# One VectorE operation per head for the row maximum and the copy of the scores to SBUF, the exponentials' bias on GpSimd, fixed PSUM tiles, and new order lists, in a thresholded attention followed by a gated MLP

## The chip, the cores and the metric

The kernel runs on one core of a Trainium2 chip. The core has a TensorE (PE), a VectorE (DVE), a ScalarE (ACT), a GpSimd (POOL) and a SyncE (SP), whose queue issues most of the DMAs. Each engine works through its own queue in order and waits on semaphores for the others. The metric is the device time of one execution in microseconds (us), the median over several runs.

## What is computed

```python
def _attn_ref(q, k, v, tau):                      # 8 batches, 8 heads, 576 rows, 64 wide
    scores = (1.0 / np.sqrt(64)) * np.matmul(q, k.transpose(0, 1, 3, 2))
    thresh = np.max(scores, axis=-1, keepdims=True) - tau          # tau = 0.02
    scores = np.where(scores >= thresh, scores, -1000000000.0)
    scores = scores - np.max(scores, axis=-1, keepdims=True)
    attn = np.exp(scores)
    attn = attn / (np.sum(attn, axis=-1, keepdims=True) + 1e-09)
    return np.matmul(attn, v)

def _moe_ref(x, w_in, w_spatial, b_spatial, w_out):  # x: heads side by side, 512 wide
    h = np.maximum(x @ w_in, 0.0)
    u, v = h[..., :512], h[..., 512:]
    v_n = (v - mean(v)) / np.sqrt(var(v) + 1e-06)
    v_s = np.einsum('ts,bsd->btd', w_spatial, v_n) + b_spatial[None, :, None]
    return (u * v_s) @ w_out
```

Only scores within tau of their row's maximum keep a weight; the weights are normalised by the sum of those kept.

## The kernel before

**Groups.** The 64 heads are taken in 32 pairs, and the rows of a pair in blocks of 128 (the last 64 rows of two pairs share a block), which makes 144 groups of 128 rows x 2 heads x 576 scores, 18 to a batch. A group `g` goes through these steps, each named by a letter in the order lists:

- `S`, `Y` (`scores`, `scores_end`, both through `part`, L819): PE multiplies, and the scores land in one of two PSUM tiles, `s_ring[g % 2]`, each three banks long.
- `G` (`turn_bank`, L834): an empty instruction of ACT, DVE or POOL that hands the middle bank from the one head to the other.
- `M` (`top`, L853): DVE takes the maximum of both heads in one reduction over 128x1152 scores in PSUM and writes it, negated, into a corner of the same PSUM tile.
- `B` (`shift`, L859): DVE turns it into `negm`, the exponentials' bias (maximum, scale and threshold in one), two numbers a row.
- `E`, `F` (`spread`): ACT reads the scores of a head from PSUM with that bias and writes one of three SBUF tiles, `e_ring[g % 3]`. `WAYS` says in which of two ways. In way `n` it is an exponential into fp16 (L874), after which `C` (`keep`, L896) makes a bit mask of what is at least 1 and `A` (`pick`, L905) applies it, both on DVE. In way `a` it is a Prelu in fp32 with a huge slope below the threshold (L877), after which `Z` (`exps`, L912) takes the exponential of both heads on ACT. Either way the weights end in fp16 in `p_ring`. Of the 144 groups 48 go by `n` and 96 by `a`.
- `T` (`turn_p`, L917): a DMA transposes the weights; `RP` does it on PE for a few.

`P`, `i`, `p` (L494 to L537) multiply the transposed weights with V, whose extra column of ones gives the sums, and DVE divides. The result is turned (`X`, `XP`) and goes through the MLP one batch later: `v` (L645), `u` (L712), `s` (L741), `o` (L770).

**Around it.** `QA`, `QB`, `QR` transpose q and k on PE (L437, L456); `qa`, `qb`, `qr` copy the result from PSUM to SBUF on ACT or, with a `d` in front, on DVE (`evict`, L409 to L419). POOL rearranges the loaded q, k and v (L296, L323, L329), copies a 64x64 block for each pair (L449) and normalises the MLP's `v` (L685 to L697).

**Order.** Nothing schedules at run time: `ORDER` has one list of tokens for each batch (`E6:1` is step `E` of group 6 of the batch before), and the program is issued in just that order, so that the lists fix what stands behind what in every engine's queue. `LAST` does the same for the end.

**PSUM.** Six of eight banks hold the two score tiles (pool `ps_s`). The other two (`ps_f`, tiles `f`) take all other products in turn, through `bank`. After the last scores `ps_s` is closed and its six banks serve the end as tiles `t`.

The score tile of group `g` is therefore written by PE, read by DVE, written in a corner and read again by DVE, read twice by ACT, and then written by PE for group `g + 2`.

Of the kernel before, what the change touches and what calls it, by code (L numbers as in the profile page):

```python
# [9 lines left out]
F32 = mybir.dt.float32  # L10
# [24 lines left out]
(  # L35
# [18 lines left out]
(  # L54
# [120 lines left out]
WAYS = [  # L175
    "nananaanananaaanaa",
    "naaaaanananaaanaaa",
    "anaaaaannnaaaaanaa",
    "aaaannnanaaaaaanaa",
    "aaaaaannannnaanaaa",  # L180
    "anaaannannanaanaan",
# [1065 lines left out]
```

## Time and profile before

| | before |
|---|---|
| median of 3 runs | 434.13 us |
| lowest, highest | 432.89, 435.9 us |
| profiled execution | 432.44 us, its span 430.4 us |
| mean granted clock of TensorE | 0.996 |
| instructions in the profile | 12955 |
| ACT, busy share of the span | 381.8 us (89%), 575 instructions |
| POOL, busy share of the span | 170.6 us (40%), 374 instructions |
| HBM read, written | 32.79 MB, 9.44 MB |

The span is the part of the execution that the profile covers; 2.0 us of the profiled execution lie outside it. The profile gives the busy time of each engine, groups of like instructions (with count, busy time, mean length of one, and what the engine waited for ahead of them), waits by who waited for whom, and a timeline. `PEld` is TensorE's weight load, which runs beside the matmuls. A busy time is a union: where the next instruction begins before the one ahead of it has ended, the overlap counts once.

### The profile page before, as it was taken

How to read it: one execution, taken by the hardware profiler on the slowest of the kernel's cores; microseconds unless marked ns; L12 is line 12 of the kernel's file. 1: busy time of each engine (PE TensorE's matmuls, PEld its weight loads, DVE VectorE, ACT ScalarE, POOL GpSimd, SP SyncE). 2: the span in 40 equal slices, each digit the busy share in tenths (PEclk: the TensorE clock that was granted, in tenths of full speed). 3: DMA queues.
4: the chain of work that ended last, by engine and by line, in shares of the span. 5: the costliest groups of instructions: out<-in, count | busy, mean ns of one | idle time of the engine just before them, and what ended most of it. 6: DMA issues, size and time to landing. Idle time of an engine off the chain costs nothing.

```text
span 430.4 us, 12955 instructions
## 1 busy us (share of the span) xinstructions
PE 411.2 (96%) x5028; PEld 252.6 (59%) x5028; DVE 380.0 (88%) x693; ACT 381.8 (89%) x575; POOL 170.6 (40%) x374
## 2 busy tenths in 40 slices
PE   7688899999999999999999999999999999999995
PEld 3456665566745566575664667555665656564742
DVE  6989999989989989989899999998889998999662
ACT  4989999999999998999998999989999989999262
POOL 1263455483117513481334720467024540265020
PEclk9989999999999999999999999999999999999999
DMA  7998999999999999999989999999999999688823
GB/s 198 255 237 177 223 256 220 200 197 218 223 221 213 230 230 234 230 173 277 205 171 238 227 204 185 200 204 241 245 209 181 175 229 212 150 135 215 158 75 120
DMA packets 224700, 88.16 MB, mean 205 GB/s; under 512 B 195648, under 2 KB 220352, under 8 KB 224640
## 3 DMA queue, kind: packets, MB, share of 16 engines
q1 hardware_dynamic: 224192, 86.75, 99.6%
q8 instruction: 40, 0.66, 0.6%
q10 hardware_dynamic: 368, 0.33, 0.2%
q0 software_dynamic: 80, 0.26, 0.2%
q14 instruction: 20, 0.16, 0.1%
HBM read 32.79 MB, written 9.44 MB: 98 GB/s over the span
## 4 chain that ended last, share of the span: by engine, by line
PE 72%; DVE 11%; ACT 8%; issue 4%; DMA 2%; POOL 2%; DVEq 0%; POOLq 0%; ACTq 0%
PE s L819 28%; DVE s L853 7%; PE f L741 6%; PE f L499 5%; PE f L712 5%; PE f L437 5%; PE f L645 4%; PE f L770 4%; ACT e L874 3%; ACT e L877 2%; PE f L494 2%; PE f L630 2%; DMA xT<-xn 1%; PE f L456 1%; DMA uT<-in_moe_w_spatial_dram 1%
## 5 line engine op out<-in xcount | busy, mean ns | idle before, releaser
L853 DVE TENSOR_REDUCE s<-s 128x2 f32<-128x1152 f32 x144 | 195.9, 1361 | 19.5 <-PE s L819 17.0
L819 PE MATMUL s<-qkT 64*64 64x416 f32 (+1 forms) x2304 | 177.8, 417 | 9.6 <-ACT e L874 5.4
L819 PEld LDWEIGHTS s<-qkT 64*64 64x64 f32 x2304 | 105.0, 132 | 67.9 <-ACT e L877 14.5
L877 ACT ACTIVATE e<-s,negm 128x576 f32<-128x576 f32 x192 | 132.5, 741 | 6.6 <-DVE negm L859 4.2
L912 ACT ACTIVATE p<-e 128x1152 f16<-128x1152 f32 x96 | 111.3, 1167 | 0.8
L874 ACT ACTIVATE e<-s,negm 128x576 f16<-128x576 f32 x96 | 66.3, 739 | 8.3 <-DVE negm L859 6.9
L499 PE MATMUL f<-v,pT 128*128 128x65 bf16 x984 | 44.3, 194 | 0.0
L499 PEld LDWEIGHTS <-pT 128*128 128x128 f16 x1024 | 41.8, 98 | 1.9
L323 POOL CAST v<-vl 128x512 bf16<-128x512 f32 x32 | 21.3, 666 | 52.2 <-PE s L819 38.0
L449 POOL COPY qkT<-qkT 64x64 f32<-64x64 f32 x32 | 8.6, 269 | 83.2 <-DVE qkT L413 31.1
L905 DVE TENSOR_TENSOR p<-e 128x576 int32<-128x576 int32 x48 | 39.4, 824 | 0.7 <-PE s L819 0.4
L296 POOL COPY qn<-ql 128x512 f32<-128x512 f32 x31 | 21.1, 681 | 32.3 <-PE s L819 30.8
L741 PE MATMUL f<-wsT,vn 128*128 128x512 bf16 x135 | 33.0, 380 | 0.5 <-DVE xn L537 0.5
L712 PE MATMUL f<-xT,w_in 128*128 128x512 bf16 x116 | 29.6, 380 | 0.0
L697 POOL TENSOR_SCALAR vn<-vrel,rs,nm 128x512 bf16<-128x512 f32 (+1 forms) x35 | 27.7, 792 | 3.6
L645 PE MATMUL f<-w_in,xT 128*128 128x512 bf16 x112 | 28.1, 380 | 0.7 <-ACT vrel L654 0.5
L494 PE MATMUL f<-v,pT 128*128 128x130 bf16 x123 | 27.3, 222 | 0.5 <-DVE xn L537 0.5
L537 DVE TENSOR_TENSOR xn<-f,r 128x384 bf16<-128x384 f32 x46 | 24.8, 548 | 0.8 <-PE s L819 0.3
L770 PE MATMUL f<-w_o,gT 128*128 128x512 bf16 x100 | 25.4, 380 | 0.0
L859 DVE TENSOR_SCALAR negm<-s 128x2 f32<-128x2 f32 x144 | 22.2, 154 | 3.0 <-PE s L819 0.2
L896 DVE TENSOR_SCALAR e<-e 128x1152 uint16<-128x1152 f16 x48 | 23.0, 481 | 0.0
L296 POOL COPY kn<-kl 128x512 f32<-128x512 f32 x31 | 20.4, 657 | 6.0 <-DMA kl<-in_k_dram 6.0
(171 smaller groups left out, 533.6 us busy)
## 6 DMA issues: line engine op xcount, KB each, us to landing
vl<-in_v_dram SPq DMA_DIRECT2D x16, 512.0 KB, 5.6
kl<-in_k_dram SPq DMA_DIRECT2D x15, 512.0 KB, 4.6
ql<-in_q_dram SPq DMA_DIRECT2D x15, 512.0 KB, 5.1
out_dram<-oo SPq DMA_DIRECT2D x12, 512.0 KB, 3.7
pT<-p SPq DMA_TRANSPOSE x141, 4.4
uT<-in_moe_w_in_dram SPq DMA_DIRECT2D x3, 512.0 KB, 5.6
uT<-in_moe_w_spatial_dram SPq DMA_DIRECT2D x2, 576.0 KB, 4.5
vx<-in_v_dram SPq DMA_DIRECT2D x16, 64.0 KB, 4.3
```

The source lines that it names most:

```text
L296: nc.gpsimd.tensor_copy(out=t, in_=ld_ring[i // 2 % 2][w][:, 2 * (i % 2):2 * (i % 2) + 2].rearrange("p h c d -> p c h d"))
L499: nc.tensor.matmul(out=t[:, at + 65 * h:at + 65 * h + 65], lhsT=pt[:, 5 * h + j, rows], rhs=vt[:, 6 * h + j, :], start=False, stop=(h == 1 ...
L645: nc.tensor.matmul(out=t, lhsT=x_of(b, f, slice(c * P, (c + 1) * P)), rhs=w_in[:, f, 512:1024], start=(f == 0), stop=(f == 3))
L712: nc.tensor.matmul(out=t, lhsT=w_in[:, m, f * P:(f + 1) * P], rhs=x_of(b, m, slice(0, 512)), start=(m == 0), stop=(m == 3))
L741: nc.tensor.matmul(out=t, lhsT=vn[:, c, f * P:(f + 1) * P], rhs=wsT[:, c, 0:512], start=(c == 0), stop=(c == 4))
L770: nc.tensor.matmul(out=t[:n], lhsT=gs[b][:, f, c * P:c * P + n], rhs=w_o[:, f, :], start=(f == 0), stop=(f == 3))
L819: made.append(nc.tensor.matmul(out=s_ring[g % 2][halves[k], at[h] + lo:at[h] + hi], lhsT=qks[n][halves[h], 0, m:m + 64], rhs=qks[n][halves ...
L853: nc.vector.tensor_reduce(out=nm[:, heads], in_=view(s_ring[g % 2], at[h0], dims), axis=AX.X, op=ALU.max, negate=True)
L874: nc.scalar.activation(out=half_e(g)[0][:, S * h:S * h + S], in_=s, func=ACT.Exp, bias=bias_, scale=scale if steps[g][1] == 4 else 1.0)
L877: nc.scalar.activation(out=e, in_=s, func=ACT.Prelu, bias=bias_, scale=scale if steps[g][1] == 4 else 1.0, alpha=1e30)
L905: nc.vector.tensor_tensor(out=numerators(g).bitcast(I32), in0=e.bitcast(I32), in1=kept.bitcast(I32), op=ALU.bitwise_and)
L912: nc.scalar.activation(out=numerators(g), in_=e_ring[g % 3].rearrange("p h s -> p (h s)"), func=ACT.Exp)
```

## The change

**Maximum and copy.** For each head DVE issues one `tensor_tensor_reduce`: it adds a broadcast zero to the scores in PSUM, writes the sum (the scores) in fp32 into the SBUF tile of `e_ring`, and keeps the maximum, which goes to a small SBUF tile `peak`. Each of them is built as two instructions, the operation and one that reads the accumulator out. So a group has four instructions of DVE here where it had two.

**Bias.** `shift` runs on POOL, from `peak`, with the sign in its scale.

**Exponentials.** `spread` reads the scores from `e_ring`, in place, and no longer touches PSUM. The fp16 halves of `e_ring` are laid out by head, so that L896 and L905 see two pieces of 576 in place of one of 1152.

**PSUM.** The eight banks are fixed tiles; `next_bank` hands out the two `f` banks in turn, and at the end the banks of the score tiles.

**Lists.** All of `ORDER`, `LAST` and most of `WAYS` are different. 43 groups go by way `n` and 101 by `a`. Of the copies from PSUM, 19 move from ACT to DVE: 12 of `qkT` (15 on DVE before, 27 now), three of `pT`, two of `xT`, one of `wsT`, one of `uT`. PE, POOL (but for the 144 biases) and SP issue the same operations as before in another order; there are 282 on SP before and after.

```diff
 ORDER = [(
-    "S0:0 vG0:0 Y0:0 sk1:0 L3:-1 M0:0 B0:0 L8:0 L7:0 S1:0 aG1:0 Y1:0 M1:0 B1:0 F0:0 E0:0 QR1:0 QB1:0 qr1:0 "
+    "S0:0 G0:0 Y0:0 M0:0 B0:0 F0:0 E0:0 Ci0:0 L7:0 L8:0 S1:0 vG1:0 Y1:0 M1:0 QA1:0 S2:0 sk1:0 G2:0 Y2:0 "
...
-    ps_f = ctx.enter_context(tc.tile_pool(name="ps_f", bufs=2, space=PSUM))
-    ps_s = inner.enter_context(tc.tile_pool(name="ps_s", bufs=1, space=PSUM))
-    s_ring = [ps_s.tile([P, 1536], F32, name=f"s{i}") for i in range(2)]
+    ps = ctx.enter_context(tc.tile_pool(name="ps", bufs=1, space=PSUM))
+    s_ring = [ps.tile([P, 1536], F32, name=f"s{i}") for i in range(2)]
+    f_ring = [ps.tile([P, 512], F32, name=f"f{i}") for i in range(2)]
+    def next_bank(kind):
+        n = in_turn[kind]
+        in_turn[kind] += 1
+        if kind == "f":
+            return f_ring[n % 2][:, 0:512]
+        return s_ring[n % 6 // 3][:, 512 * (n % 3):512 * (n % 3) + 512]
...
 def top(g, heads=slice(0, 2)):
-        nc.vector.tensor_reduce(out=nm[:, heads], in_=view(s_ring[g % 2], at[h0], dims), axis=AX.X,
-                                op=ALU.max, negate=True)
+        for h in range(heads.start, heads.stop):
+            nc.vector.tensor_tensor_reduce(
+                out=e_ring[g % 3][:, h, :], in0=view(s_ring[g % 2], at[h], [[1, S]]),
+                in1=zero.broadcast_to([P, S]), scale=1.0, scalar=float("-inf"),
+                op0=ALU.add, op1=ALU.max, accum_out=peak[g][:, h:h + 1])
 def shift(g):
-        nc.vector.tensor_scalar(out=nm, in0=s_ring[g % 2][:, 704:706],
-                                scalar1=scale if steps[g][1] == 4 else 1.0,
+        nc.gpsimd.tensor_scalar(out=nm, in0=peak[g],
+                                scalar1=-(scale if steps[g][1] == 4 else 1.0),
 def half_e(g):
-        t = e_ring[g % 3].rearrange("p h s -> p (h s)").bitcast(F16)
-        return t[:, 0:1152], t[:, 1152:2304]
+        t = e_ring[g % 3].bitcast(F16)
+        return t[:, :, 0:S], t[:, :, S:2 * S]
 def spread(g, h):
-        s = view(s_ring[g % 2], at[h], [[1, S]])
+        s = e_ring[g % 3][:, h, :]
...
-        inner.close()
-        wide.append(ctx.enter_context(tc.tile_pool(name="ps_t", bufs=6, space=PSUM,
-                                                  reuse_waits="tile")))
+        wide.append(True)
```

DVE's queue from the reduction of group 60 on, in the fourth batch, before (`s_94` and `s_95` are the two score tiles, `e_103` to `e_105` the three tiles of `e_ring`, `p_` those of `p_ring`):

```order
L853 TENSOR_REDUCE s_94<-s_94 128x2
L905 TENSOR_TENSOR p_114<-e_104 128x576
L859 TENSOR_SCALAR negm<-s_94 128x2
L853 TENSOR_REDUCE s_95<-s_95 128x2
L859 TENSOR_SCALAR negm<-s_95 128x2
L896 TENSOR_SCALAR e_103<-e_103 128x1152
L896 TENSOR_SCALAR e_105<-e_105 128x1152
L905 TENSOR_TENSOR p_115<-e_105 128x576
L853 TENSOR_REDUCE s_94<-s_94 128x2
L859 TENSOR_SCALAR negm<-s_94 128x2
```

The same queue from the same group on, in the changed kernel (`s_91` and `s_92` are the score tiles, `f_93` and `f_94` the other two banks; `ISA` is the new operation, and the `ISA` that writes `peak` alone its accumulator read):

```order
L862 ISA e_103,peak<-s_91,zero 128x576
L862 ISA peak 128x1
L862 ISA e_103,peak<-s_91,zero 128x576
L862 ISA peak 128x1
L769 TENSOR_TENSOR gT<-f_94,uT 128x512
L425 TENSOR_SCALAR qkT<-f_93 128x512
L862 ISA e_104,peak<-s_92,zero 128x576
L862 ISA peak 128x1
L862 ISA e_104,peak<-s_92,zero 128x576
L862 ISA peak 128x1
L427 COPY qkT<-f_94 128x512
L427 COPY oo<-f_93 128x512
```

The reduction and the bias of a group have become four instructions in a row, the bias has left the queue, and copies of `qkT` stand between the groups.

POOL's queue around one conversion of v (`v_131`) in the fourth batch, before:

```order
L685 TENSOR_SCALAR rs<-mv 128x1
L690 TENSOR_TENSOR rs<-rs,mhalf 128x1
L692 TENSOR_SCALAR nm<-mv,rs 128x1
L697 TENSOR_SCALAR vn_132<-vrel,rs,nm 128x512
L323 CAST v_131<-vl_139 128x2x4x64
L329 CAST v_131<-vx_143 64x64 x2
```

The queue around the same conversion in the changed kernel (L870 is the bias):

```order
L711 TENSOR_SCALAR vn_132<-vrel,rs,nm 128x512
L870 TENSOR_SCALAR negm<-peak 128x2
L306 COPY qn<-ql_134 128x512
L306 COPY kn<-kl_135 128x512
L870 TENSOR_SCALAR negm<-peak 128x2 x3
L333 CAST v_131<-vl_139 128x2x4x64
L339 CAST v_131<-vx_143 64x64 x2
```

The biases stand singly or in runs between the conversions of q, k and v and the MLP's normalisation.

More of the change, by code (lines that the diff above doesn't have):

```diff
@@ L20 @@
 ORDER = [(
[14 rows of a table removed]
-(
[18 rows of a table removed]
-(
[18 rows of a table removed]
-(
[18 rows of a table removed]
-(
[17 rows of a table removed]
-(
[18 rows of a table removed]
-(
[17 rows of a table removed]
-(
[16 rows of a table removed]
[14 rows of a table added]
+(
[18 rows of a table added]
+(
[19 rows of a table added]
+(
[17 rows of a table added]
+(
[18 rows of a table added]
+(
[18 rows of a table added]
+(
[17 rows of a table added]
+(
[17 rows of a table added]
 LAST = [(
-    "u3:2 eu3:2 s0:2 s1:2 T12:1 es0:2 B16:1 C15:1 A15:1 OUT3:3 sv2:1 es1:2 T13:1 E17:1 s3:2 F17:1 "),
+    "sv3:1 B16:1 E17:1 F17:1 s3:2 T13:1 es1:2 "),
 (
[4 rows of a table removed]
[3 rows of a table added]
 (
@@ L177 @@
     "naaaaanananaaanaaa",
[L178 to L181, printed above, removed]
-    "anaaaanaananaaanan",
-    "anaaaanananaaaanan",
+    "anaaaaannnaanaaaaa",
+    "aaaaaananannaaaaaa",
+    "naanaaanannnaanaaa",
+    "aaaaannaananaaanaa",
+    "aanaaanaaaanaanaaa",
+    "naaaaaanaanaannnaa",
 ]
@@ L224 @@
     sqr = ctx.enter_context(tc.tile_pool(name="sqr", bufs=1))
-    inner = ctx.enter_context(ExitStack())
-    ps_f = ctx.enter_context(tc.tile_pool(name="ps_f", bufs=2, space=PSUM))
-    ps_s = inner.enter_context(tc.tile_pool(name="ps_s", bufs=1, space=PSUM))
-    s_ring = [ps_s.tile([P, 1536], F32, name=f"s{i}") for i in range(2)]
+    ps = ctx.enter_context(tc.tile_pool(name="ps", bufs=1, space=PSUM))
+    s_ring = [ps.tile([P, 1536], F32, name=f"s{i}") for i in range(2)]
+    f_ring = [ps.tile([P, 512], F32, name=f"f{i}") for i in range(2)]
+    in_turn = {"f": 0, "t": 0}
+    def next_bank(kind):
[4 more added lines that the diff above has]
+        return s_ring[n % 6 // 3][:, 512 * (n % 3):512 * (n % 3) + 512]
     identf = const.tile([P, P], F32, name="identf")
@@ L237 @@
     mhalf = const.tile([P, 1], F32, name="mhalf")
+    zero = const.tile([P, 1], F32, name="zero")
     warm = const.tile([P, P], BF16, name="warm")
@@ L388, with shaped @@
     turn = [0]
+    def shaped(t, dtype, n):
+        return t if dtype == F32 else t.bitcast(dtype)[:, 0:n]
     def bank(dtype=F32, n=512):
@@ L394, in bank @@
             if turn[0] % 8 not in (2, 3):
-                return wide[0].tile([P, n], dtype, name="t")
-        return ps_f.tile([P, n], dtype, name="f")
+                return shaped(next_bank("t"), dtype, n)
+        return shaped(next_bank("f"), dtype, n)
     def bank16():
@@ L468, in first @@
         qkt = qk_of(0)
-        tr, tq, tm = (ps_f.tile([P, 512], F32, name="f") for _ in range(3))
+        tr, tq, tm = (next_bank("f") for _ in range(3))
         def turn(t, at, w, c):
@@ L839, in scores_end @@
         follow(part(g, 1, 0, S - cut)[0], turned[g])
-    negm = {}
+    negm, peak = {}, {}
     def top(g, heads=slice(0, 2)):
-        if on_act(g):
-            nm = s_ring[g % 2][:, 704:706]
-        elif g in negm:
-            nm = negm[g]
-        else:
-            nm = negm[g] = small.tile([P, 2], F32, name="negm")
-        h0, n = heads.start, heads.stop - heads.start
-        dims = [[at[1] - at[0], n], [1, S]] if n > 1 else [[1, S]]
-        nc.vector.tensor_reduce(out=nm[:, heads], in_=view(s_ring[g % 2], at[h0], dims), axis=AX.X,
-                                op=ALU.max, negate=True)
+        if g not in peak:
+            peak[g] = small.tile([P, 2], F32, name="peak")
+        for h in range(heads.start, heads.stop):
[3 more added lines that the diff above has]
+                op0=ALU.add, op1=ALU.max, accum_out=peak[g][:, h:h + 1])
     def shift(g):
         nm = negm[g] = small.tile([P, 2], F32, name="negm")
-        nc.vector.tensor_scalar(out=nm, in0=s_ring[g % 2][:, 704:706],
-                                scalar1=scale if steps[g][1] == 4 else 1.0,
+        nc.gpsimd.tensor_scalar(out=nm, in0=peak[g],
+                                scalar1=-(scale if steps[g][1] == 4 else 1.0),
                                 scalar2=float(tau) + (0.0 if way(g) == "a" else half_step),
@@ L864, in half_e @@
     def half_e(g):
-        t = e_ring[g % 3].rearrange("p h s -> p (h s)").bitcast(F16)
-        return t[:, 0:1152], t[:, 1152:2304]
+        t = e_ring[g % 3].bitcast(F16)
+        return t[:, :, 0:S], t[:, :, S:2 * S]
     def spread(g, h):
-        s = view(s_ring[g % 2], at[h], [[1, S]])
+        s = e_ring[g % 3][:, h, :]
         e, bias_ = e_ring[g % 3][:, h, :], negm[g][:, h:h + 1]
         if way(g) in "nrs":
-            nc.scalar.activation(out=half_e(g)[0][:, S * h:S * h + S], in_=s, func=ACT.Exp,
+            nc.scalar.activation(out=half_e(g)[0][:, h, :], in_=s, func=ACT.Exp,
                                  bias=bias_, scale=scale if steps[g][1] == 4 else 1.0)
@@ L904, in pick @@
         if way(g) == "n":
-            nc.vector.tensor_tensor(out=numerators(g).bitcast(I32), in0=e.bitcast(I32),
+            nc.vector.tensor_tensor(out=numerators(g).rearrange("p (h s) -> p h s", h=2).bitcast(I32), in0=e.bitcast(I32),
                                     in1=kept.bitcast(I32), op=ALU.bitwise_and)
         else:
-            nc.gpsimd.tensor_tensor(out=numerators(g), in0=e, in1=kept, op=ALU.mult)
+            nc.gpsimd.tensor_tensor(out=numerators(g).rearrange("p (h s) -> p h s", h=2), in0=e, in1=kept, op=ALU.mult)
     def exps(g):
@@ L1171 @@
         clear()
+        nc.vector.memset(zero, 0.0)
         nc.vector.memset(ntau, -float(tau))
@@ L1183 @@
         for _ in range(7):
-            nc.tensor.matmul(out=ps_f.tile([P, 512], F32, name="f").rearrange(
+            nc.tensor.matmul(out=next_bank("f").rearrange(
                 "p (a b) -> p a b", a=4), lhsT=warm,
```

279 rows, old and new, of tables (LAST, ORDER) are left out of this document.

## The prediction

> **What bounds the kernel now.** I read the page's busy shares and its chain first, then the long middle stretch alone, then who waits for whom in it, and then the groups that the change touches. From the page, busy time with its share and instruction count, and the engines' shares of the chain that ended last:
>
> ```profile
> PE 411.2 (96%) x5028; PEld 252.6 (59%) x5028; DVE 380.0 (88%) x693; ACT 381.8 (89%) x575; POOL 170.6 (40%) x374
> ...
> PE 72%; DVE 11%; ACT 8%; issue 4%; DMA 2%; POOL 2%; DVEq 0%; POOLq 0%; ACTq 0%
> ```
>
> The windows 10 to 400 us, where the attention groups run, and 400 to the end (length, then busy time of PE, PEld, DVE, ACT, POOL, the granted clock, DMA share, GB/s):
>
> ```profile
> 10.00:400.00 390.00, 377.63 (x4696) 234.10 (x4697) 358.54 (x629) 366.35 (x545) 165.11 (x360) 1.00 1.06 212
> ...
> 400.00:430.40 30.40, 25.82 (x284) 14.52 (x280) 14.77 (x40) 11.87 (x24) 3.31 (x5) 1.00 0.44 112
> ```
>
> In the middle stretch PE shows 97%, ACT 94% and DVE 92%. No engine alone is the bound: three nearly full queues hand each other work through two score tiles, and what is lost is waiting. DVE stands still for 390.0 - 358.5 = 31.5 us there, ACT for 23.7 us. The waits, longest first (total, times, longest):
>
> ```profile
> DVE s L853 <- PE s L819: 17.0, 39, 1.0
> PEld s L819 <- ACT e L877: 14.5, 32, 0.9
> PEld s L819 <- ACT e L874: 12.3, 23, 1.8
> ACT e L874 <- DVE negm L859: 6.9, 12, 2.4
> PE s L819 <- ACT e L874: 5.4, 8, 1.5
> ACT e L877 <- DVE negm L859: 4.2, 14, 0.7
> PE s L819 <- ACT e L877: 3.8, 9, 0.6
> DVE r L534 <- PE f L499: 2.9, 6, 0.7
> DVE qkT L413 <- PE f L456: 1.6, 5, 0.5
> ```
>
> These are one ring read at three places: PE's scores wait for ACT's exponentials of two groups before (9.2 us in PE's own rows), DVE's maximum waits for the scores (17.0), and ACT waits for the bias (11.1).
>
> **The change part by part.** The groups it touches, by shape (busy us, mean ns of one, then idle time ahead and who ended it):
>
> ```profile
> L853 DVE TENSOR_REDUCE s<-s 128x2 f32<-128x1152 f32 x144 | 195.9, 1361 | 19.5 <-PE s L819 17.0 <-ACT o L660 0.4 <-ACT uT L415 0.3
> ...
> L877 ACT ACTIVATE e<-s,negm 128x576 f32<-128x576 f32 x192 | 132.5, 741 | 6.6 <-DVE negm L859 4.2 <-PE s L819 0.6 <-DVE mv L668 0.4
> ...
> L912 ACT ACTIVATE p<-e 128x1152 f16<-128x1152 f32 x96 | 111.3, 1167 | 0.8
> ...
> L905 DVE TENSOR_TENSOR p<-e 128x576 int32<-128x576 int32 x48 | 39.4, 824 | 0.7 <-PE s L819 0.4
> ...
> L896 DVE TENSOR_SCALAR e<-e 128x1152 uint16<-128x1152 f16 x48 | 23.0, 481 | 0.0
> ...
> L697 POOL TENSOR_SCALAR vn<-vrel,rs,nm 128x512 bf16<-128x512 f32 x28 | 21.5, 768 | 2.9
> L323 POOL CAST v<-vl 128x512 bf16<-128x512 f32 x32 | 21.3, 666 | 52.2 <-PE s L819 38.0 <-PE f L770 8.5 <-PE f L513 4.9
> ...
> L755 DVE TENSOR_TENSOR gT<-f,uT 128x512 bf16<-128x512 f32 x27 | 18.3, 682 | 0.8 <-PE f L741 0.4
> ...
> L417 ACT ACTIVATE qkT<-f 128x512 f32<-128x512 f32 x23 | 13.8, 600 | 2.4 <-POOL bias L384 1.4 <-PE f L437 0.7
> ...
> L685 POOL TENSOR_SCALAR rs<-mv 128x1 f32<-128x1 f32 x22 | 4.9, 221 | 17.5 <-DVE mv L668 9.9 <-PE f L645 2.6 <-DVE negm L859 2.1
> ...
> L678 ACT ACTIVATE sq<-vrel,nmean 128x512 bf16<-128x512 f32 x6 | 4.3, 711 | 0.0
> ```
>
> DVE's timeline in the middle (start, length), for what an instruction costs from start to start, and ACT's around an accumulator read near the end:
>
> ```profile
> 237.23 0.68 DVE L664 BATCH_NORM_STATS2 st<-vrel 128x6 f32<-128x512 f32 x1
> 237.83 1.35 DVE L853 TENSOR_REDUCE s<-s 128x2 f32<-128x1152 f32 x1
> 239.22 0.16 DVE L859 TENSOR_SCALAR negm<-s 128x2 f32<-128x2 f32 x1
> 239.29 0.17 DVE L668 BATCH_NORM_AGGREGATE mv<-st 128x2 f32<-128x6 f32 x1
> 239.38 0.66 DVE L664 BATCH_NORM_STATS2 st<-vrel 128x6 f32<-128x512 f32 x1
> 240.01 1.37 DVE L853 TENSOR_REDUCE s<-s 128x2 f32<-128x1152 f32 x1
> 241.28 0.17 DVE L668 BATCH_NORM_AGGREGATE mv<-st 128x2 f32<-128x6 f32 x1
> ```
>
> ```profile
> 414.03 0.19 ACT L982 ACTIVATION_READ_ACCUMULATOR sq<-vrel,nmean 128x1 f32 x1
> 414.12 0.58 ACT L415 ACTIVATE uT<-f 128x512 bf16<-128x512 f32 x1
> ```
>
> *Removed from DVE.* A reduction followed by its own bias takes 239.22 - 237.83 = 1.39 us to the bias and 0.07 more to the next start: 1.46. Where another instruction stands between them, the reduction takes 241.28 - 240.01 = 1.27 and the bias 0.07 to 0.08: 1.35. I take the middle, 1.41 us a group.
>
> *Added to DVE.* No row is the new operation. The nearest is the two-input multiplication from PSUM, 682 ns for 512 elements. DVE's slope from the reduction is (1361 - 682) / (1152 - 512) = 1.06 ns an element, so 576 take about 0.75 us. The next one starts 0.08 before the end (237.23 to 237.83 is 0.60 for a 0.68 us instruction), so each costs 0.67. The accumulator read has no row on DVE either. Its ends are 0 (hidden in the pipe) and 0.19 (a whole ACT read after the operation has drained, which adds the 0.08 of lost overlap: 0.27). The nearest row is ACT's read, which holds the next start back by 0.09; DVE's tiny instructions take 0.07 to 0.09. I take 0.08. A group is then 2 x (0.67 + 0.08) = 1.50 us, between 1.34 and 1.88. Against 1.41 that is +0.09, times 144: **+13 us** of DVE, between -10 and +68.
>
> The Trainium skill ("VectorE: DVE Perf Modes", section "The DRAIN you can't avoid") says that the next DVE operation does not start until the pipe is empty. The rows above show starts 0.08 us ahead of the end, and the same section names such starts for instructions that are not held; what a full drain would give is the second rival below.
>
> *Masks and copies.* Five groups leave way `n`: 5 x (0.481 + 0.824 - 0.16 of overlap) = 5.7 us less on DVE, 5 x 1.167 = 5.8 more on ACT. The 19 copies that move to DVE cost it 0.60 each, +11.4 us, and spare ACT 19 x 0.60 = 11.4. The layout of L896 and L905 in two pieces keeps the count of elements; I cost it at nothing, with the inner run still 576 long.
>
> *Exponentials from SBUF.* ACT's row with a bias from SBUF is 711 ns for 512 elements. With ACT's slope between that and L912, (1167 - 711) / (1152 - 512) = 0.71 ns, 576 elements take 757 ns against 741 from PSUM: +16 ns, times 288, +5 us of ACT. The lower end is 0; with DVE's slope of 1.06 it is 779 ns and +11 us at the most. So ACT: 366.4 + 5 + 5.8 - 11.4 = 366 us in the stretch, as now.
>
> The Trainium skill ("VectorE: DVE Perf Modes", section on the TRN2 errata) gives ScalarE a fixed cost of 224 cycles from SBUF and 172 from PSUM, which speaks against the change. As an estimate from that page, 52 cycles at its 1.2 GHz are 43 ns, 12.5 us in all, and ACT would stand at 373; DVE would still be the fuller one.
>
> *The bias on POOL.* 144 x 0.22 us = 32 us of POOL, which has 225 us free in the stretch. A bias can stand behind a conversion or a normalisation; ACT's exponentials wait for it, and the e tile is held longer. It is hidden as long as the maximum runs ahead of ACT, and with the score tile freed by DVE it can run up to three groups ahead (three e tiles) where it had two score tiles. That it fails is the third rival.
>
> *PE.* The same matmuls. A score tile is now free when DVE has read it, so PE's 9.2 us of waiting for exponentials has no cause left, and the 17.0 us that DVE waits for scores should go with it, since PE can refill one tile while DVE spends 1.5 us on the other; of the 2.9 + 1.6 us that DVE waits for other products, which stand behind those scores in PE's queue, I take 3. SP's transfers move with the lists, but they are as many, and no DMA is among the long waits above.
>
> *The sum.* DVE in the stretch: 358.5 + 13 - 5.7 + 11.4 = 377.2 busy, and 31.5 - 17 - 3 = 11.5 idle, together 388.7 against 390.0. The rest of the span stays at 40.4. That is 1.3 us less, 431.1 for the profiled execution of 432.4. The median shown is 1.7 above that execution, so the sum stands for 432.8; I go to **431.5** because the lists are rewritten around the freer tiles and ACT's 11.1 us of waits on the bias can shrink too. What the loosened ring gives, a fuller DVE takes back.
>
> **The rivals.**
>
> *All waits of the ring go, and the read is hidden.* DVE takes 1.34 a group, is 354 busy, and ACT ends last: 366 + 23.7 - 11.1 = 379 in the stretch, 11 less, 423 us. PE's 377.6 us of busy time leaves no more. For it: the waits all lie in the ring that is opened. Against: it needs the lower end of a price that I put at 0.08.
>
> *DVE becomes the bound: slower.* The accumulator read waits for the operation to end. At 0.16 a read (the length of DVE's own small instructions) a group takes 1.66, +36 us, and the stretch 358.5 + 36 + 5.7 + 11.5 = 412, 22 more: 456. At 0.12 it is 445. It decides from a read of about 0.10 on, where the stretch passes 394. For it: the bias behind its reduction waits for the end (1.39 against 1.27), and a read depends on its operation in the same way. Against: ACT's read does not. By the skill's rule of the full drain each group would cost 2 x (0.75 + 0.16) = 1.82, at this end or beyond it.
>
> *The bias comes late.* POOL is busy 165 of 390 us, most of it in pieces of 0.67 to 0.77 (L323, L697). A bias that finds it busy waits some 0.3: 144 x 0.42 x 0.3 = 18 us, and the semaphore's way is added. If half shows in ACT's queue, ACT has 366 + 23.7 + 9 = 399, and the time is 443. Against: three e tiles give ACT something else to do.
>
> **How the numbers follow.** The forecast (425 to 437) gets 0.45, all waits gone (423) 0.22, DVE the bound (445 to 467) 0.21, the late bias (443) 0.12. About 1%, 4.3 us, is what a measurement of this kernel can tell from no change: 429.8 to 438.5. Of the forecast's 0.45 I give 0.15 to below 429.8 and 0.30 to the middle, of the late bias 0.06 to the middle. Faster: 0.15 + 0.22 = 0.37; same: 0.36; slower: 0.21 + 0.06 = 0.27. The range runs from 420 to 447, leaving out the far part of the second rival and little below; the forecast's own is 425 to 437.
>
> **What would show it.** The new operation at 0.75 us and its read at 0.07 to 0.09 from start to start; DVE at 97% of the stretch, ACT at 94 to 95%; exponentials of 0.76 us; PE's scores no longer waiting for ACT but, if at all, for DVE; DVE's wait for the scores well below 17 us. Wrong it is if the read costs over 0.1, if ACT's waits on the bias exceed 11 us, or if DVE waits long for an e tile.

## The result, and the profile after

| | before | after |
|---|---|---|
| median | 433.93 us (4 runs) | 448.34 us (4 runs) |
| lowest, highest | 432.89, 435.9 us | 447.11, 453.1 us |
| ratio, 95% interval | | 1.0347, 1.026 to 1.0434 |
| span of the profiled execution | 430.4 us | 445.5 us |

The changed kernel is 3.5% slower, beyond the upper end of the range. One of ten executions of a later kernel, e8, took 659.69 us at a granted clock of 0.56; it is left out of its median, and its profile, which is of that execution, is not read. The page's busy shares and its chain of the changed kernel:

```profile
PE 414.2 (93%) x5028; PEld 256.6 (58%) x5028; DVE 379.6 (85%) x991; ACT 384.7 (86%) x561; POOL 203.6 (46%) x518
...
PE 52%; DVE 15%; ACT 9%; DMA 7%; POOL 7%; issue 6%; SPq 1%; POOLq 0%; DVEq 0%; ACTq 0%
```

DVE has as much work as before (380.0 us there), and of the engines only POOL has distinctly more. PE's share of the chain fell from 72 to 52%, DMA's rose from 2 to 7%, POOL's from 2 to 7%. The span is 15.1 us longer, and but for POOL's that is not more work, it is waits. Where they lie is told by cutting both spans at the same events: the start of the first maximum and the end of the last. First the stretch between them before (columns as in the prediction), then after:

```profile
7.34:395.29 387.95, 375.27 (x4681) 232.90 (x4674) 356.65 (x621) 363.56 (x541) 165.25 (x360) 1.00 1.06 213
```

```profile
9.12:401.16 392.04, 374.98 (x4685) 235.44 (x4678) 357.71 (x924) 365.46 (x527) 198.50 (x504) 1.00 1.02 210
```

So 9.12 - 7.34 = 1.8 us are lost ahead of the first maximum, 392.0 - 388.0 = 4.1 in the middle, and at the end (445.5 - 401.2) - (430.4 - 395.3) = 44.3 - 35.1 = **9.2**. The 1.8 us at the start are in part chance: kernels below whose lists start in the same way have their first maximum between 7.40 (e9) and 9.80 us (e13), and kernels with the old lists between 7.34 and 8.00 (e14).

The groups that were changed, by shape (busy us, mean ns, idle ahead):

```profile
L862 DVE CUSTOM_DVE_ANT_0 e<-s,zero 128x576 f32<-128x576 f32 x288 | 204.5, 751 | 19.6 <-PE s L833 6.8 <-issue 2.7 <-DVE p L916 1.6
L888 ACT ACTIVATE e<-e,negm 128x576 f32<-128x576 f32 x202 | 146.4, 766 | 12.3 <-POOL negm L870 12.1
...
L885 ACT ACTIVATE e<-e,negm 128x576 f16<-128x576 f32 x86 | 63.3, 768 | 6.3 <-POOL negm L870 5.9
...
L870 POOL TENSOR_SCALAR negm<-peak 128x2 f32<-128x2 f32 x144 | 32.1, 223 | 147.6 <-DVE peak L862 100.4 <-DVE r L548 9.8 <-ACT p L923 7.2
L862 DVE DVE_READ_ACCUMULATOR2_ANT peak<- 128x1 f32 x288 | 23.6, 82 | 0.0
```

DVE's timeline (start, length) shows what a head costs from start to start:

```profile
230.72 0.08 DVE L862 DVE_READ_ACCUMULATOR2_ANT peak<- 128x1 f32 x1
230.72 0.75 DVE L862 CUSTOM_DVE_ANT_0 e<-s,zero 128x576 f32<-128x576 f32 x1
231.40 0.08 DVE L862 DVE_READ_ACCUMULATOR2_ANT peak<- 128x1 f32 x1
231.40 0.45 DVE L907 TENSOR_SCALAR e<-e 128x1152 uint16<-128x1152 f16 x1
```

A read starts in the same moment as the instruction behind it. Operation and read together take 231.40 - 230.72 = 0.68 us, a group 1.36. The waits among the engines, longest first:

```profile
POOL negm L870 <- DVE peak L862: 100.4, 63, 3.9
...
ACT e L888 <- POOL negm L870: 12.1, 15, 2.3
...
DVE r L548 <- PE f L513: 8.1, 8, 2.7
ACT vl L1048 <- PE s L1046: 7.3, 2, 6.2
...
PEld s L833 <- DVE peak L862: 7.2, 18, 1.4
DVE e L862 <- PE s L833: 6.8, 12, 1.9
ACT uT L429 <- PE s L513: 6.6, 1, 6.6
...
ACT e L885 <- POOL negm L870: 5.9, 7, 3.5
...
PEld L508 <- DMA pT<-p: 2.8, 3, 1.3
```

PE's scores wait no more for ACT's exponentials and Prelus (L885, L888), and DVE's wait for scores fell from 17.0 to 6.8 us, as the prediction has it. Others came in: ACT for the bias (18.0, was 11.1), DVE for the products of the weights with V (8.1, was 2.9), PE and its loads for transposed weights (8.7 in all, was 0.2), and a few long ones at the end (`vl`, `uT`). All the idle time ahead of DVE's maximum is 19.6 us, as it was before (19.5): what the scores no longer cost there, other short waits do, on POOL, ACT and DVE itself among them.

### The profile page after: what moved, and what is told of

The parts are those of the page before. It is cut to its first block, busy times and chain, and to the rows that moved or that the text cites. A ratio compares the mean times of both kernels' runs of the same rounds, so it can differ in the third digit from the quotient of the medians.

```text
span 445.5 us, 13371 instructions
## 1 busy us (share of the span) xinstructions
PE 414.2 (93%) x5028; PEld 256.6 (58%) x5028; DVE 379.6 (85%) x991; ACT 384.7 (86%) x561; POOL 203.6 (46%) x518
## 4 chain that ended last, share of the span: by engine, by line
PE 52%; DVE 15%; ACT 9%; DMA 7%; POOL 7%; issue 6%; SPq 1%; POOLq 0%; DVEq 0%; ACTq 0%
PE s L833 21%; DVE e L862 8%; DMA pT<-p 7%; PE f L755 5%; PE f L513 5%; PE f L451 4%; ACT e L888 3%; PE f L726 3%; PE f L659 2%; ACT p L923 2%; PE f L784 2%; PE f L508 2%; ACT e L885 1%; DVE p L916 1%; SPq L928 1%
## 5 line engine op out<-in xcount | busy, mean ns | idle before, releaser
L862 DVE CUSTOM_DVE_ANT_0 e<-s,zero 128x576 f32<-128x576 f32 x288 | 204.5, 751 | 19.6 <-PE s L833 6.8
L888 ACT ACTIVATE e<-e,negm 128x576 f32<-128x576 f32 x202 | 146.4, 766 | 12.3 <-POOL negm L870 12.1
L833 PEld LDWEIGHTS s<-qkT 64*64 64x64 f32 x2304 | 106.6, 133 | 55.0 <-issue 18.7
L923 ACT ACTIVATE p<-e 128x1152 f16<-128x1152 f32 x101 | 116.4, 1157 | 0.9
L870 POOL TENSOR_SCALAR negm<-peak 128x2 f32<-128x2 f32 x144 | 32.1, 223 | 147.6 <-DVE peak L862 100.4
L885 ACT ACTIVATE e<-e,negm 128x576 f16<-128x576 f32 x86 | 63.3, 768 | 6.3 <-POOL negm L870 5.9
L513 PE MATMUL f<-v,pT 128*128 128x65 bf16 x984 | 44.5, 194 | 0.0
L513 PEld LDWEIGHTS <-pT 128*128 128x128 f16 x1024 | 42.0, 98 | 4.2 <-issue 2.2
L916 DVE TENSOR_TENSOR p<-e 128x576 int32<-128x576 int32 x43 | 33.7, 784 | 0.9 <-DVE peak L862 0.2
L755 PE MATMUL f<-wsT,vn 128*128 128x512 bf16 x135 | 32.6, 380 | 0.1
L508 PE MATMUL f<-v,pT 128*128 128x130 bf16 x123 | 27.2, 221 | 4.3 <-DMA pT<-p 2.5
L862 DVE DVE_READ_ACCUMULATOR2_ANT peak<- 128x1 f32 x288 | 23.6, 82 | 0.0
L726 PEld LDWEIGHTS <-w_in 128*128 128x128 bf16 x128 | 11.8, 99 | 16.8 <-issue 6.2
```

Of the source, the lines that this page charges most:

```text
L508: nc.tensor.matmul(out=t[:, at:at + 130], lhsT=pt[:, 4, rows], rhs=vt[:, 4:6, :].rearrange("p b d -> p (b d)"), start=True, stop=False)
L513: nc.tensor.matmul(out=t[:, at + 65 * h:at + 65 * h + 65], lhsT=pt[:, 5 * h + j, rows], rhs=vt[:, 6 * h + j, :], start=False, stop=(h == 1 ...
L726: nc.tensor.matmul(out=t, lhsT=w_in[:, m, f * P:(f + 1) * P], rhs=x_of(b, m, slice(0, 512)), start=(m == 0), stop=(m == 3))
L755: nc.tensor.matmul(out=t, lhsT=vn[:, c, f * P:(f + 1) * P], rhs=wsT[:, c, 0:512], start=(c == 0), stop=(c == 4))
L833: made.append(nc.tensor.matmul(out=s_ring[g % 2][halves[k], at[h] + lo:at[h] + hi], lhsT=qks[n][halves[h], 0, m:m + 64], rhs=qks[n][halves ...
L862: nc.vector.tensor_tensor_reduce(out=e_ring[g % 3][:, h, :], in0=view(s_ring[g % 2], at[h], [[1, S]]), in1=zero.broadcast_to([P, S]), scal ...
```

## The experiments

### The end: one tile of three banks, or three tiles

My first theory was that the end pays for its banks being slices of the two score tiles, since a reader of a slice then waits for whatever PE writes last into any bank of that tile. In e1 the changed kernel gets its six banks at the end as tiles of their own again (the score tiles are in a pool that is closed first); in e2 the kernel before gets slices.

```diff
--- changed kernel
+++ e1_end_tiles
-        return s_ring[n % 6 // 3][:, 512 * (n % 3):512 * (n % 3) + 512]
+        return wide[0].tile([P, 512], F32, name="t")[:, 0:512]
-        wide.append(True)
+        inner.close()
+        wide.append(ctx.enter_context(tc.tile_pool(name="ps_t", bufs=6, space=PSUM,
+                                                  reuse_waits="tile")))
--- kernel before
+++ e2_end_slices
-                return wide[0].tile([P, n], dtype, name="t")
+                k = wide.append(True) or len(wide) - 2
+                t = s_ring[k % 6 // 3][:, 512 * (k % 3):512 * (k % 3) + 512]
```

> The changed kernel, with one part of it undone: after the last scores the six banks are tiles of their own again (score tiles released, pool of six one-bank tiles), not slices of the two three-bank score tiles. Theory of the end (a slice waits for everything that was issued earlier on the other slices of its tile): from the end of the last maximum to the end of the span 35 us in place of 44.3, the middle as it is, so about 439 us. Rival (the new lists for the end are at fault): the end stays at 43 to 45 us and the time at 446 to 449.

> The kernel before, with only this changed: after the last scores the six banks are handed out as slices of the two score tiles; lists, operations and the f tiles are those of before. Theory of the end: 35.1 us from the last maximum to the end become 42 to 45, and the time 441 to 444. Rival (the lists): 433 to 435, the end at 35 us.

Measured: e1 437.9 us (ratio to the kernel before 1.008, 1.0055 to 1.0105), e2 444.06 us (1.0219, 1.0175 to 1.0263). Taking the slices away gives 10.4 us back, putting them in costs 10.1 (433.93 to 444.06). Both lie at the end. From the end of the last maximum to the end of the span the changed kernel takes 44.3 us and e1 34.2; the kernel before takes 35.1 and e2 45.3, while e2's middle stays at 387.9. (The profiled execution of e1 is the longest of its ten, 441.87 us, so its middle is not read here; e19 below is the same kernel.) The mechanism stands in the timeline of the changed kernel:

```profile
402.85 1.28 DVE L769 TENSOR_TENSOR gT<-f,uT 128x512 bf16<-128x512 f32 x2
402.94 1.24 PE L755 MATMUL s<-wsT,vn 128*128 128x512 bf16 x5
...
405.00 0.41 PE L513 MATMUL s<-v,pT 128*128 128x65 bf16 x8
405.45 0.69 DVE L769 TENSOR_TENSOR gT<-s,uT 128x512 bf16<-128x512 f32 x1 [1.32 <-PE s L513]
...
411.88 0.38 ACT L429 ACTIVATE uT<-s 128x256 bf16<-128x256 f32 x1 [6.61 <-PE s L513]
```

The product that L769 reads (L755) ends at 402.94 + 1.24 = 404.18, but the reader waits until PE has ended L513 at 405.41, which writes another bank of the tile. `uT` waits 6.61 us in the same way, also until an L513 has ended. With tiles of their own (e1) the same instruction starts straight behind the one ahead of it, with no wait:

```profile
407.63 1.28 DVE L771 TENSOR_TENSOR gT<-f,uT 128x512 bf16<-128x512 f32 x2
409.00 0.69 DVE L771 TENSOR_TENSOR gT<-t,uT 128x512 bf16<-128x512 f32 x1
```

### The operations under the old lists

Next the operations without the new lists. e4 is the kernel before with only the bias on POOL, and e8 its control: the maxima go to SBUF in the same way, but the bias stays on DVE. e3 is the kernel before with all new operations under the old lists (in 21 of 144 groups the steps of group g - 3 that read the e tile are issued ahead of the maximum that overwrites it), and e6 is e3 with the bias on DVE.

```diff
--- kernel before
+++ e4_bias_pool
-            nm = s_ring[g % 2][:, 704:706]
+            peak[g] = small.tile([P, 2], F32, name="peak")
...
-        nc.vector.tensor_scalar(out=nm, in0=s_ring[g % 2][:, 704:706],
+        nc.gpsimd.tensor_scalar(out=nm, in0=peak[g],
--- e4_bias_pool
+++ e8_bias_sbuf_dve
-        nc.gpsimd.tensor_scalar(out=nm, in0=peak[g],
+        nc.vector.tensor_scalar(out=nm, in0=peak[g],
--- e3_ops_old_lists
+++ e6_bias_dve_old_lists
-        nc.gpsimd.tensor_scalar(out=nm, in0=peak[g],
+        nc.vector.tensor_scalar(out=nm, in0=peak[g],
```

> The kernel before with the new operations alone (copy and maximum in one DVE operation per head, bias on GpSimd, exponentials from SBUF), its own lists, WAYS and PSUM pools; where a list has the maximum of a group ahead of the last step that reads the e tile of three groups before (21 of 144 groups), that step is issued ahead of the maximum. Theory of the late bias: ACT waits for the bias over 18 us in all, more than the 11 us before, and the time is 437 to 445. Rival (the operations are fine and the new lists cost the middle its time): 427 to 433, with DVE waiting for scores well under 17 us.

> The kernel before with only the bias moved: the reduction writes its two maxima to SBUF and GpSimd makes the bias; the exponentials still read PSUM. Theory of the late bias: the score tile is now held for the way through GpSimd as well, so PE's and DVE's waits in the ring grow by 0.15 to 0.3 us in most groups, and the time is 443 to 460, although DVE is spared 22 us of work. Rival (the way through GpSimd costs nothing): 430 to 434.

> The kernel of e3_ops_old_lists (new operations under the lists of before) with the bias back on DVE. Theory of the late bias (of e3's 112 us all come from the bias that stands behind other work in GpSimd's queue): 426 to 436, ACT's waits for the bias near the 11 us of before, DVE's waits for scores under 10 us, since the score tile is free before the exponentials. Rival (the copy by DVE, or the 21 steps issued earlier, cost the lists of before as much): 445 or more, with DVE waiting long for an e tile.

> Kernel before; as in e4_bias_pool the reduction writes the maxima to a small SBUF tile, but the bias stays on DVE, at its old place, and reads them there. Theory (all of e4's 94 us come from POOL's place in the line: a bias queued behind conversions and normalisations): 432 to 437 us, no wait of ACT for the bias above the 11 us of before. Rival (what costs is writing the maxima to SBUF in place of a corner of the PSUM tile, by a dependence that this adds): 445 us or more.

Measured: e3 546.65 us (1.2577, 1.2519 to 1.2636), e4 528.58 us (1.2169, 1.2113 to 1.2226), e6 468.53 us (1.08, 1.075 to 1.0851), e8 436.0 us (1.0055, 1.0031 to 1.0079). I had the sign of e3 and e4 but missed their size by some 70 to 100 us; in e6 the rival holds (445 us or more); e8 came as expected in its time. So writing the maxima to SBUF costs 2 to 3 us, and moving the bias from DVE to POOL 93 (528.58 - 436.0). POOL's timeline in e4, with the bias (L856) at its ends:

```profile
174.57 0.19 POOL L856 TENSOR_SCALAR negm<-peak 128x2 f32<-128x2 f32 x1 [1.36 <-DVE mv L668]
174.83 0.61 POOL L296 COPY qn<-ql 128x512 f32<-128x512 f32 x1
...
184.44 0.76 POOL L697 TENSOR_SCALAR vn<-vrel,rs,nm 64x512 bf16<-64x512 f32 x1
...
185.59 0.47 POOL L856 TENSOR_SCALAR negm<-peak 128x2 f32<-128x2 f32 x2
```

Two biases of 0.2 us stand behind 11 us of copies and a whole normalisation. ACT waits for such biases 51.3 + 31.6 us in all of e4:

```profile
ACT e L874 <- POOL negm L856: 51.3, 33, 6.1
...
ACT e L871 <- POOL negm L856: 31.6, 21, 3.3
```

PE's mean granted clock also falls, to 0.94 in e3 and e4, and its busy time grows from 411.2 us to 452.9 and 445.3; how much of the 93 us that is, no run separates. In e6 the bias is out of POOL's queue, and a new wait comes up, that of DVE's maximum and copy for L910, ACT's exponential of both heads:

```profile
DVE e L849 <- ACT p L910: 35.5, 25, 2.8
```

The e tile is taken from the maximum on, and no longer from the first exponential on. Whether the 21 steps that are issued earlier cost a part of e6's time as well stays open.

### Bias, copies and e tiles under the new lists

From here all is counted from e1, 437.9 us. e5 has the bias on DVE, e9 has it twice on POOL (once into a spare tile), e11 has 22 of DVE's copies of `qkT` on ACT again (every other such token of the lists). e10 has four e tiles; for their room it has nine tiles of weights in place of ten, and e12, its control, has those nine and three e tiles (the second pair of lines alone). With nine, some weights are overwritten before they are read, so e10 and e12 multiply other weights in some groups.

```diff
--- e1_end_tiles
+++ e5_bias_dve_new_lists
-        nc.gpsimd.tensor_scalar(out=nm, in0=peak[g],
+        nc.vector.tensor_scalar(out=nm, in0=peak[g],
--- e1_end_tiles
+++ e9_bias_twice
-        nc.gpsimd.tensor_scalar(out=nm, in0=peak[g],
+        for t in (spare, nm):
+            nc.gpsimd.tensor_scalar(out=t, in0=peak[g],
--- e1_end_tiles
+++ e11_copies_on_act
-dqa1:0
+qa1:0
...
--- e1_end_tiles
+++ e10_four_e_tiles
-    e_ring = [const.tile([P, 2, S], F32, name=f"e{i}") for i in range(3)]
+    e_ring = [const.tile([P, 2, S], F32, name=f"e{i}") for i in range(4)]
-    p_ring = [const.tile([P, 1152], F16, name=f"p{i}") for i in range(10)]
+    p_ring = [const.tile([P, 1152], F16, name=f"p{i}") for i in range(9)]
```

> The kernel of e1_end_tiles (the changed one, its last six banks tiles of their own) with the bias back on DVE, from the maxima in SBUF. Theory of the late bias (ACT's 18 us of waits for GpSimd's bias are what the middle has lost): these waits fall under 8 us, and the time is 428 to 434, although DVE gets 10 to 20 us of small instructions more. Rival (DVE has no room for them, and the waits of the middle come from the queues' order): 438 to 448.

> Kernel e1_end_tiles (437.9 us), with each bias computed twice on POOL, first into a spare tile, then into the real one; POOL gets 144 x 0.22 = 32 us more, and each bias comes 0.2 us later. Theory (the changed lists still let the late bias cost time: it is the 18 us of ACT's waits on POOL that hold the e tiles): between 0.1 and 0.25 us a group come through, 450 to 470 us with ACT's waits on POOL at 35 us or more. Rival (the late bias is covered by the three e tiles, and the rest of the slowdown is DVE's and the score ring's): 437 to 441 us.

> Kernel e1_end_tiles (437.9 us), with 22 of the copies of qkT that the changed lists give to DVE done by ACT, in the same places of the lists: DVE 22 x 0.6 = 13 us less busy, ACT 13 us more. Theory (ACT is late because it waits for a bias, and cannot take more work): 443 to 452 us. Rival (DVE is the bound, its price of the new operations being what slows the middle): 430 to 436 us.

> Kernel e1_end_tiles (437.9 us), with four e tiles in place of three and, to make room for the fourth, nine tiles of weights in place of ten. Theory (an e tile is held from the copy on, so three of them are too few: the maximum of group g+3 cannot be written before group g is done): 430 to 435 us, DVE's and ACT's idle time down together. Rival (the lists already place the maximum after the e tile is free, so that the order and not the tile sets the distance): 436 to 440 us, unchanged.

> Control for e10_four_e_tiles: kernel e1_end_tiles (437.9 us) with nine tiles of weights in place of ten, and three e tiles as before. If the 467 us of e10_four_e_tiles came from the nine tiles alone, this gives 460 to 475 us, and a fourth e tile is worth what it differs from 467; if the fourth e tile did it, 436 to 442 us.

Measured: e5 457.18 us (1.0541, 1.0501 to 1.058), e9 446.52 us (1.0295, 1.0264 to 1.0326), e11 449.11 us (1.0344, 1.0304 to 1.0383), e10 467.39 us (1.0777, 1.0742 to 1.0812), e12 471.09 us (1.0851, 1.081 to 1.0891). Under the new lists neither engine takes more work for nothing: in e11 8.6 us of busy time move from DVE (379.8 to 371.2) to ACT, fewer than the 13 that I expected, and cost 11, as the theory had it; in e5 the bias back on DVE costs 19, beyond both the theory and the rival, ACT now waiting 40 us for it. On POOL 32 us more cost 8.6 (e9), 0.06 a group, between my theory's 0.1 to 0.25 and the rival's next to nothing: the late bias is partly covered, not wholly. e10 fits neither of its two expectations, and e12 tells why: the nine tiles alone cost 33 us. With a fourth e tile it is 3.7 us less, hardly more than the runs can tell (the intervals touch), and what that tile would be worth beside ten tiles of weights stays open.

### The middle: transposed weights behind loads

These runs tell what the engines can bear, not what the 4 us are. The larger DMA share of the chain led there: the transposes of the weights (`T`) go through SP's queue, and at the end of the third batch the chain of waits of the changed kernel (start, length) runs through it into a product with V (L508):

```profile
138.87 0.28 POOL negm L870
139.15 0.13 SPq L290
...
139.33 1.39 SPq L928
...
140.77 0.58 SPq L281
...
141.40 1.28 SPq L928
...
142.72 7.32 DMA pT<-p
...
150.09 0.23 PE f L508
```

L281 is a load of q of 512 KB, L290 one of v, which itself was released by POOL. The load of q was issued ahead of a transpose (L928), and that lands only after 7.32 us, where the median of all is 4.2. (The Trainium skill, "DMA: Bandwidth & Descriptors", section "Queues, rings and completion order", says that the descriptors of a ring are consumed in order; the 7.32 us fit that, and do not test it.) e13 leaves out 12 stores to lighten the transfers, e14 is its control on the kernel before. e15 moves six loads behind the transposes that follow them, and nothing else; one of them, in batch 1, then stands behind a step that reads it, so that rows of q in that batch are old ones. e16 is e15 without that move, and e19 is e1 again on the same chip. In the lists of e16 `L8:-1` stands behind `T7:0` instead, and `L9:0` and `L6:-1` behind `T13:1`, the last transposes of their runs.

```diff
--- e1_end_tiles
+++ e13_no_stores
-            nc.sync.dma_start(out=rows[:, c - 1:c + 1, :], in_=pair_o[b, c // 2])
--- e1_end_tiles
+++ e16_loads_behind_t
-N2:1 L5:-2 T10:0 L7:-1 T8:0 T7:0 L6:-2
+N2:1 T10:0 T8:0 T7:0 L5:-2 L7:-1 L6:-2
-T9:0 L8:-1 T6:0 T3:0
+T9:0 T6:0 T3:0
-T11:1 L9:0 X0:1 T15:1 T16:1 L6:-1 G2:0
+T11:1 X0:1 T15:1 T16:1 G2:0
```

> Kernel e1_end_tiles (437.9 us) without the 12 stores of the MLP's output pairs (512 KB each), so that those rows of the output stay unwritten; the transfers take 6 of 88 MB less. Theory (what is left of the slowdown in the middle is PE waiting for transposed weights behind other transfers, 8.7 us of PE and its loads in the changed kernel, next to nothing before): 432 to 435.5 us. Rival (the transfers are hidden, the rest is waits among the engines): 437 to 439 us.

> Control: kernel before without the same 12 stores, so that those rows of the output stay unwritten. PE waits 0.2 us for transposed weights there, so by the theory nothing is gained: 432.5 to 434.5 us. If it gains as much as e13_no_stores does, the stores cost something else than late weights.

> Kernel e1_end_tiles (437.9 us) with six loads of q, k and v moved in SP's queue behind the transposes of weights that stand right behind them, at the four places where PE waits for transposed weights (in the batches 1, 2, 3 and 6); the other queues stay as they are. Theory (those transposes land late because a load of 512 KB is ahead of them): PE's waits for pT fall from 6.5 us to under 2.5, and the time to 433 to 436 us. Rival (weights that are late on ACT or DVE, or full transfer engines whatever the order): waits for pT unchanged, 437 to 439 us. Loads that now come too late would show as POOL or DVE waiting for ql, kl or vl, and 438 us or more.

> Kernel e1_end_tiles once more, beside the next three on the same chip: 436.5 to 438.5 us, the value from which they are counted.

> As e15_loads_behind_t, without its move in batch 1 (which put a load of q behind a step that reads it): five loads moved in SP's queue, in the batches 2, 3 and 6. Theory (these transposes were late because loads stood ahead of them): 1.5 to 3 us below e19_end_tiles_again, PE's waits for pT under 3 us, and 0.2 to 0.7% left above the kernel before. Rival (the gain of e15_loads_behind_t was chance between chips): within 1 us of e19_end_tiles_again.

Measured: e13 435.21 us (1.0038, 1.0017 to 1.006), e14 433.42 us (0.9993, 0.9974 to 1.0011), e15 435.11 us (1.0042, 1.0017 to 1.0067); then, on one chip, e19 437.72 us (1.0089, 1.0056 to 1.0122) and **e16 433.56 us (0.9993, 0.997 to 1.0016)**. The stores cost the kernel before nothing, and e1 2.5 us (e13 against e19). Moving five loads gives 4.2 us, all that was left, and more than the 1.5 to 3 that I expected. Of the 4.2 the two profiled executions show 2.4 in the middle (393.2 us in e19, 390.8 in e16) and nothing at the end (33.9 and 34.0). The waits for transposed weights in e19, then in e16, where they are 2.0 us in all in place of 7.0:

```profile
PEld L510 <- DMA pT<-p: 1.9, 2, 1.6
PEld L523 <- DMA pT<-p: 1.8, 1, 1.8
PE f L523 <- DMA pT<-p: 1.7, 1, 1.7
PE f L510 <- DMA pT<-p: 1.6, 2, 1.4
```

```profile
PEld L510 <- DMA pT<-p: 1.1, 2, 0.8
PE f L510 <- DMA pT<-p: 0.9, 2, 0.7
```

The transposes still land after 2.8 to 8.4 us in e16, as in e19: what changed is how early they are issued, not the slowest landing. At the place shown above PE now finds its weights in time (`x5` are transposes that two loads had split):

```profile
135.60 8.31 SPq L930 DMA_TRANSPOSE pT<-p  x5
144.01 0.67 SPq L292 DMA_DIRECT2D vx<-in_v_dram  x1
144.72 0.60 SPq L283 DMA_DIRECT2D ql<-in_q_dram  x1
...
148.60 0.22 PE L510 MATMUL f<-v,pT 128*128 128x130 bf16 x1
```

### The relays

One more suspect was the relay of the middle bank: 70 of them stand in POOL's queue behind biases that wait for DVE. e17 sends the 14 at which PE waited longest through ACT's queue, e18 through DVE's (`vG3:0`).

```diff
--- e16_loads_behind_t
+++ e17_relays_act
-G3:0
+aG3:0
...
```

> As e16_loads_behind_t, and at the 14 groups at which PE waited longest for a bank relay in POOL's queue (6.2 us of weight loads in all) that relay goes through ACT's queue. Theory (relays stand in POOL's queue behind biases that wait for DVE, and this is the other part of what is left): 1 to 2 us below e16_loads_behind_t, at or below the kernel before. Rival (ACT's queue makes them as late, or PE's wait there is covered by DVE): within 1 us of e16_loads_behind_t, or above it.

> As e17_relays_act, with the 14 relays in DVE's queue. Theory: 1 to 2 us below e16_loads_behind_t. Rival: within 1 us of it, or above, where a relay stands behind a maximum that itself waits for scores.

Measured: e17 435.31 us (1.0031, 1.0005 to 1.0058), e18 439.27 us (1.0128, 1.0087 to 1.0169). PE's longest waits for relays, first in e16, where the 14 stand in POOL's queue:

```profile
PEld s L835 <- POOLq L850: 4.9, 12, 1.0
PE s L835 <- POOLq L850: 1.1, 3, 0.6
```

Then in e17 (ACT's queue) and in e18 (DVE's queue):

```profile
PEld s L835 <- ACTq L850: 3.1, 8, 0.7
```

```profile
PEld s L835 <- DVEq L850: 5.5, 12, 1.5
```

PE and its loads wait 9.1 us for all relays in e16, 5.9 in e17 and 7.5 in e18. So the waits became shorter in both, and both are slower, by 1.7 and 5.7 us. The rival holds, but not because the relays come as late as before: shorter waits gain nothing here, so they do not set the time. What makes the two kernels slower these runs do not show.

## Why the prediction was wrong

- *The step that failed most: "The rest of the span stays at 40.4".* I did not cost the fixed PSUM tiles at the end at all, though the diff shows them. The end took 44.3 us in place of 35.1, and the fixed tiles are 10 us of the time (e1 and e2, from both sides). They hold no more data and no more work; a tile of three banks is waited for as one.
- *The second: "SP's transfers move with the lists, but they are as many, and no DMA is among the long waits above".* True of the kernel before, and no evidence on the lists to come. Five loads of q, k and v ahead of transposes are worth 4.2 us (e16 against e19). With the 10.4 of the first step that is the whole of the 14.4 us that the change costs. I had looked at the queues of DVE and POOL, and not at SP's.
- *The price of the new operation.* Mis-sized: 1.36 us a group, near the lower end of 1.34, where I took 1.50. The read is hidden, so the term of +13 us comes out as (1.36 - 1.41) x 144 = -7, and DVE in all went from 380.0 to 379.6 us, where my terms gave 13 - 5.7 + 11.4 = +19. By the rule of the Trainium skill ("VectorE: DVE Perf Modes", section "The DRAIN you can't avoid") a group would have cost an estimated 1.82; the operations here start 0.07 us before the one ahead of them has ended.
- *The waits of the ring.* PE's for the exponentials went and DVE's for scores fell by 10.2 us where I took 17.0, but DVE's idle time in the middle is 392.0 - 357.7 = 34.3 us, not 11.5. DVE's busy time was taken some 19 us too high and its idle time some 23 too low. The sum has the middle 1.3 us shorter, it came out 4.1 longer; that it is no further off is luck. The step that failed here took idle time that one wait gives up as gone: ahead of the maximum it is 19.6 us as before, in other waits, and DVE waits 5.2 us longer for the products, where I had taken 3 off.
- *Exponentials from SBUF.* 766 ns against 741 for the same Prelu (L877) before: 25 ns each, where I took 16. The estimate of 43 ns from the fixed costs that the Trainium skill gives ("VectorE: DVE Perf Modes", section "The TRN2 errata — SBUF-src ops pay a fixed extra latency per instruction") is too high for this kernel.
- *The bias on POOL.* "Hidden" holds only by the grace of the lists: 93 us under the old ones (e8 to e4). Under the new ones ACT's 18.0 us for it are past the 11 that I named as the sign of being wrong, but under these lists the place is still cheaper than DVE (e5).
- *What held.* Without the two defects the change neither gains nor loses (e16: 433.56 us), near the forecast, but not for the reason given, that a fuller DVE takes back what the loosened ring gives: DVE is no fuller. In e16 the waits that came in are ACT's for the bias (16.0 us, was 11.1) and DVE's for the products (7.8, was 2.9); that these are what takes the gain back is read from the profile, and no run isolates it. None of the rivals was the cause: the read did not make DVE the bound, and e16 loses nothing with the bias still on POOL.

No kernel here beats the kernel before by more than its measurement can tell. e16 equals it, and is 14.8 us below the changed kernel with the same operations on every engine.

## What to carry over

Cost every part of a diff in the stage in which it runs, the short last stage too: two lines on how PSUM is cut into tiles cost more than the operation that the change is about, because tiles are what waits are counted by. Where an order is rewritten, read every queue, the transfers' above all, and ask of each short transfer which long one is now issued ahead of it. And an engine with half its time free is no free place for a small operation on the critical chain: its queue decides, not its load.

## What the runs showed of the hardware

The read of the accumulator costs DVE nothing that shows from start to start: the next operation starts 0.68 us after one of 0.75 us, the read of 0.08 us between them included. The same bias takes 223 ns on POOL from SBUF (L870 above), 217 on DVE from SBUF and 154 on DVE from PSUM; the two on DVE stand behind different operations, so the place of the data need not be the whole difference. The groups of e5, then of the kernel before:

```profile
L872 DVE TENSOR_SCALAR negm<-peak 128x2 f32<-128x2 f32 x144 | 30.0, 217 | 2.4
```

```profile
L859 DVE TENSOR_SCALAR negm<-s 128x2 f32<-128x2 f32 x144 | 22.2, 154 | 3.0 <-PE s L819 0.2
```

The busy share of the 16 DMA engines is counted as 1.06 before and 1.02 after in the windows from 10 to 400 us. A transpose of weights lands after 2.8 to 8.5 us in the changed kernel (3.2 to 8.2 before). That a load ahead of them makes the weights late is shown only for the five loads moved in e16.
